# Block-causal attention and a gated MLP on one core: the posts of the v groups in another order

## The chip, the cores and the metric

The kernel runs on one core of a Trainium2 chip. The time is the device time of one execution in microseconds (us), as a median of several. The core has a matrix engine (TensorE, PE in the profile, with PEld for its weight loads), VectorE (DVE), ScalarE (ACT), GpSimd (POOL) and SyncE (SP), which issues most DMAs. Every engine works through its own list of instructions in order and waits on semaphores for the others.

## The reference

Attention over 8 batches, 8 heads, 576 tokens, 64 columns a head, with a mask by blocks of 64; its output, heads joined to 512 columns, goes through a gated MLP:

```python
scores = where(block_i >= block_j, q @ k.T / 8, -1e9)
attn = softmax(scores)                        # exp(s - max) / (sum + 1e-9)
x = join_heads(attn @ v)                      # 576 x 512 a batch
h = maximum(x @ w_in, 0)                      # 576 x 1024
u, v = h[..., :512], h[..., 512:]
v_n = (v - mean(v)) / sqrt(var(v) + 1e-6)     # by token
v_s = w_spatial @ v_n + b_spatial             # 576 x 576, over tokens
out = (u * v_s) @ w_out                       # 512 x 512
```

## The kernel before

Two heads make a pair, so a batch has four pairs (`pr` 0 to 3), and the program has 32 (`g`). The attention of one batch and the MLP of the batch before it are woven together. For each pair the main loop first issues all scores (L592, `scores_run`), which VectorE masks and takes the maximum of (L416), ScalarE exponentiates (`p`, L423) and GpSimd scales (L514); then the product with v of the pair before (`av_pair`, L676), which ScalarE casts and VectorE splits into high and low parts (`x`, L327 and L329). VectorE transposes p in blocks (`pb`, L631 and L638), and SP's DMAs regroup them into `ptt` (L652, L660) for the next `av`. Rows 512 and up of both heads make set 8 (L444 to L495).

Between these stand groups of the MLP, seven or eight to a pair. Matrix products use numbers split in two, so a product is three passes. The groups:

- `v_group(c)`, c from 0 to 4: the matmuls (`mv`, L719, for c = 4 L730), the emptying of the PSUM bank (`vr`, L724), then posts. The posts are the variance (L741, L742), on ScalarE 1/sqrt by Ln and Exp (L744, L745), four small products one column wide that polish it and give the shift (L747, L751, L755, L759, tile `st`), and last the scaling of `vr` (L764), its high part `vh` (L770) and on GpSimd its low part `vl` (L771). For c = 4 the parts are `vs_a` and `vs_b` (L776 to L778).
- `u_group`: the matmuls `mu` (L791) and the bank's emptying (L796).
- `sp_group`: `ms` (L821 to L826), which needs all `vh` and `vl`; then `out_group`: `mo` (L847).

A group is a Python generator. `issue` starts a new one, which emits its matmuls and empties its bank, and calls `follow`, which gives every group in the list `behind` one more step up to its next `yield`. So the `yield`s and the calls of `follow` set the place of the posts in every engine's list. From step 28 on, `issue` starts the new group first and calls `follow` after it. At the last group of pairs 0 and 1 `issue` leaves `follow` out, and it is called once between the products of the next pair's `av` and the transposes (L1049). What has been emitted is then chained with `in_order`, so each engine's list is exactly the order of emission.

The groups by pair, in batches 2 to 7 (the MLP is then that of the batch before): pair 0 has the last four `mo` and v0, v4, u; pair 1 has v1, u, v2, u, v3, u, u; pair 2 has the last three u and four `ms`; pair 3 four `mo` and four `ms`. In the MLP of batch 0 and in that of the last batch, which has no attention beside it, the order is another.

PSUM banks of tag `m` are two and serve all MLP groups in turn; six others in a ring (`bank`) serve scores and `av`. Of `vr` there are three buffers. `pb` and `ptt` are single.

Of the kernel before, what the change touches and what calls it, by code (L numbers as in the profile page):

```python
# [55 lines left out]
def kernel(  # L56
# [10 lines left out]
    nc = tc.nc  # L67
    B, NPAIR = qk.shape[0], qk.shape[1]
# [7 lines left out]
    FULL = S // P  # L76
# [98 lines left out]
    step = 0  # L175
# [342 lines left out]
    def scores_8(b, pr):  # L518
        raw = raws[(b, pr)]
        st = stats[(b, pr)] = st_p.tile([P, 52], F32, tag="sst", name=f"sst_{b}_{pr}", bufs=3)  # L520
        ps = [bank(f"s8_{b}_{pr}_{hd}") for hd in range(2)]
        matmuls_8(raw, ps)
        top_8(st, ps)
        yield
        norm_8(st)
        yield
# [50 lines left out]
    def scores_run(b, pr):  # L577


        raw = raws.pop((b, pr))  # L580
        st = stats.pop((b, pr))
        ps = {}
        for t in (3, 2, 1, 0):
            for hd in range(2):
                js = slice(64 * hd, 64 * hd + 64)
                n = P * (t + 1)
                if t:
                    bk = bank(f"s{t}_{b}_{pr}_{hd}")
                    ps[(t, hd)] = bk[:, :n]
                    if t == 1:  # L590
                        ps[(0, hd)] = bk[:, n:n + P]
                mm(  # L592
                    ps[(t, hd)], raw[js, S + t * P:S + (t + 1) * P], raw[js, :n],
                    start=True, stop=True,
                )
        due = None
        for ts in ((3,), (2,), (1, 0)):
            tiles = []
            for hd in range(2):
                p = (p_big if ts[0] == 3 else p_small)(f"p{ts[0]}_{b}_{pr}_{hd}")  # L600
                at = 0
                for t in ts:
                    n = P * (t + 1)
                    p_of[(b, pr, t, hd)] = p[:, at:at + n]
                    top(st, t, hd, p[:, at:at + n], [ps[(t, hd)]])
                    tiles.append((t, hd, p[:, at:at + n]))
                    at += n
            if due:
                norm(st, due)
            due = tiles  # L610
        turn_blocks(b, pr, 8, 0)
        turn_blocks(b, pr, 3, 0)
        norm(st, due)
# [84 lines left out]
    def moe(b):  # L698
# [10 lines left out]
        def v_group(c):  # L709
            ps = ps_m.tile([P, 512], F32, tag="m", name=f"mv_{b}_{c}")  # L710
            vr = ff_p.tile([P, DH], F32, tag="vr", name=f"vr_{b}_{c}", bufs=3)
            st = st_p.tile([P, 16], F32, tag="st", name=f"st_{b}_{c}")
            cs = slice(c * P, min((c + 1) * P, S))
            n = 0
            if c < FULL:
                m = P
                for k in range(NC):
                    for j, w in ((0, wi_hi), (0, wi_lo), (1, wi_hi)):
                        mm(  # L719
                            ps, xs[k][:, j, cs], w[:, k, DH:],  # L720
                            start=(n == 0), stop=(n == 3 * NC - 1),
                        )
                        n += 1
                nc.scalar.activation(vr, ps, AF.Relu)  # L724
            else:

                m = S - FULL * P
                for k in range(NC):
                    for w in (wi_hi, wi_lo):
                        mm(  # L730
                            ps, xs_tail[:, k].rearrange("p j t -> p (j t)"), w[:, k, DH:],
                            start=(n == 0), stop=(n == 2 * NC - 1),
                        )
                        n += 1
                nc.scalar.copy(vr[:m, :], ps[m:2 * m, :])
                nc.vector.tensor_tensor(out=vr[:m, :], in0=ps[:m, :], in1=vr[:m, :], op=ALU.add)
                nc.vector.tensor_scalar(
                    out=vr[:m, :], in0=vr[:m, :], scalar1=0.0, scalar2=None, op0=ALU.max
                )
            yield  # L740
            nc.vector.bn_stats(out=st[:m, 0:6], in_=vr[:m, :])  # L741
            nc.vector.bn_aggr(out=st[:m, 6:8], in_=st[:m, 0:6])  # L742
            yield
            nc.scalar.activation(st[:m, 8:9], st[:m, 7:8], AF.Ln, bias=eps[:m, :])  # L744
            nc.scalar.activation(st[:m, 9:10], st[:m, 8:9], AF.Exp, scale=-0.5)  # L745
            yield
            nc.vector.tensor_scalar(  # L747
                out=st[:m, 10:11], in0=st[:m, 7:8], scalar1=EPS_LN, scalar2=-0.5,
                op0=ALU.add, op1=ALU.mult,
            )  # L750
            nc.vector.tensor_scalar(  # L751
                out=st[:m, 11:12], in0=st[:m, 9:10], scalar1=st[:m, 9:10], scalar2=st[:m, 10:11],
                op0=ALU.mult, op1=ALU.mult,
            )
            nc.vector.tensor_scalar(  # L755
                out=st[:m, 12:13], in0=st[:m, 11:12], scalar1=1.5, scalar2=st[:m, 9:10],
                op0=ALU.add, op1=ALU.mult,
            )
            nc.vector.tensor_scalar(  # L759
                out=st[:m, 13:14], in0=st[:m, 6:7], scalar1=st[:m, 12:13], scalar2=-1.0,  # L760
                op0=ALU.mult, op1=ALU.mult,
            )
            yield
            nc.scalar.activation(  # L764
                vr[:m, :], vr[:m, :], AF.Identity, bias=st[:m, 13:14], scale=st[:m, 12:13]
            )
            if c < FULL:
                vh = ff_p.tile([P, DH], F32R, tag=f"vh{c}", name=f"vh_{b}_{c}")
                vl = ff_p.tile([P, DH], F32R, tag=f"vl{c}", name=f"vl_{b}_{c}")
                nc.scalar.copy(vh, vr)  # L770
                nc.gpsimd.tensor_tensor(  # L771
                    out=vl, in0=vr, in1=vh.bitcast(F32), op=ALU.subtract
                )
                vn[c] = (vh, vl)
            else:
                nc.vector.tensor_copy(vs_b[:m, :], vr[:m, :])  # L776
                nc.scalar.copy(vs_a[:m, :], vr[:m, :])
                nc.vector.tensor_tensor(  # L778
                    out=vs_a[64:64 + m, :], in0=vr[:m, :], in1=vs_b[:m, :].bitcast(F32),
                    op=ALU.subtract,  # L780
                )
# [17 lines left out]
        g = {}  # L799
# [112 lines left out]
    def next_step():  # L912
        nonlocal step
        for f in steps.pop(step, []):
            f()
        step += 1
        in_order()
# [37 lines left out]
    for n, (g, ts) in enumerate(sets):  # L955
# [21 lines left out]
        for f, tg in due:  # L977
            e = f(*pairs[tg], ps_m.tile([P, 512], F32, tag="m", name=f"av_{tg}"))
# [40 lines left out]
    behind = []  # L1019

    def follow():

        for e in list(behind):
            if next(e, e) is e:
                behind.remove(e)

    def issue(f, last=False):

        gen = f()
        if not last and step < 28:  # L1030
            follow()
        next(gen)
        if not last and step >= 28:
            follow()
        behind.append(gen)
        next_step()
# [3 lines left out]
    for g in range(NPAIR, len(pairs)):  # L1040
        b, pr = pairs[g]
        if g > NPAIR:
            scores_run(b, pr)
            av = av_pair(*pairs[g - 1])
            next(av, None)
            turn_blocks(b, pr, 3, 1)
            next(av, None)
            next(av, None)
            follow()  # L1049
            turn_blocks(b, pr, 2, 0)  # L1050
        regroup_8(b, pr)
        in_order()
        if pr == 0:
            if g > NPAIR:
                mlp = moe(b - 1)
            groups, rest = rest + mlp[0], mlp[-1]
        else:
            groups = mlp[pr]
        ahead = scores_8(*pairs[g + 1]) if g + 1 < len(pairs) else iter([])
        for i, f in enumerate(groups):  # L1060
            issue(f, pr < 2 and i == len(groups) - 1)
            if i == 0:
                turn_blocks(b, pr, 1, 0)
                turn_blocks(b, pr, 0, 0)
                turn_blocks(b, pr, 2, 1)
                turn_blocks(b, pr, 1, 1)
                turn_blocks(b, pr, 0, 1)
            if i == 1:
                regroup(b, pr)
            if i >= len(groups) - (4 if pr == 0 and g > NPAIR else 3):  # L1070
                next(ahead, None)
        in_order()
        if g + 1 < len(pairs):
            load_v(*pairs[g + 1])
        if g + 2 < len(pairs):
            load_pair(*pairs[g + 2])
        in_order()
# [61 lines left out]
```

## Time and profile before

| | us |
|---|---|
| median of 3 runs | 686.53 (686.02 to 687.38) |
| profiled execution | 685.92 |
| its span, first to last instruction | 683.8 |
| PE busy | 658.2 (96%) |
| DVE, ACT, POOL busy | 489.1, 390.3, 284.4 |
| one middle batch (309.56 to 389.76) | 80.20 |

A row of the timeline gives start, duration, engine, line, operation, output and inputs, shapes, count, and in brackets the engine's idle time before it with what ended it. `PE mu L791 <- ACT u L796: 5.1, 7, 2.8` in the list of waits reads: PE stood still before matmuls of line 791 until line 796 on ScalarE was done, 5.1 us in all, seven times, 2.8 us at the longest. The rows on the middle batch come from the MLP of batch 3, woven with the attention of batch 4.

### The profile page before, as it was taken

How to read it: one execution, taken by the hardware profiler on the slowest of the kernel's cores; microseconds unless marked ns; L12 is line 12 of the kernel's file. 1: busy time of each engine (PE TensorE's matmuls, PEld its weight loads, DVE VectorE, ACT ScalarE, POOL GpSimd, SP SyncE). 2: the span in 40 equal slices, each digit the busy share in tenths (PEclk: the TensorE clock that was granted, in tenths of full speed). 3: DMA queues.
4: the chain of work that ended last, by engine and by line, in shares of the span. 5: the costliest groups of instructions: out<-in, count | busy, mean ns of one | idle time of the engine just before them, and what ended most of it. 6: DMA issues, size and time to landing. Idle time of an engine off the chain costs nothing.

```text
span 683.8 us, 15564 instructions
## 1 busy us (share of the span) xinstructions
PE 658.2 (96%) x5328; PEld 554.3 (81%) x5328; DVE 489.1 (72%) x1899; ACT 390.3 (57%) x1144; POOL 284.4 (42%) x472
## 2 busy tenths in 40 slices
PE   8888889999999999999999999999999999999998
PEld 5545778888888887987789888888888887899998
DVE  6989898778966687776866788666877668661520
ACT  5877775456744476555654557534765556542632
POOL 4768566443443245442253434433354423540130
PEclk9999999999999999999999999999999999999999
DMA  6534664674557744566555545576445665442002
GB/s 234 169 136 151 193 145 121 179 184 112 134 137 180 180 109 102 154 165 160 140 133 141 149 125 146 132 185 174 95 110 157 152 173 150 111 112 62 0 1 70
DMA packets 51106, 93.45 MB, mean 137 GB/s; under 512 B 5970, under 2 KB 27986, under 8 KB 51028
## 3 DMA queue, kind: packets, MB, share of 16 engines
q1 hardware_dynamic: 41812, 83.03, 47.3%
q10 hardware_dynamic: 9216, 9.44, 4.2%
q8 instruction: 42, 0.69, 0.4%
q14 instruction: 36, 0.29, 0.1%
HBM read 37.13 MB, written 9.44 MB: 68 GB/s over the span
## 4 chain that ended last, share of the span: by engine, by line
PE 62%; DVE 22%; ACT 6%; POOL 5%; issue 3%; DMA 1%; SPq 0%; DVEq 0%; POOLq 0%; ACTq 0%
PE mo L847 15%; PE ms L821 13%; PE mv L719 8%; PE s L592 6%; PE mu L791 6%; PE av L676 5%; DVE p L416 4%; DVE pb L638 3%; POOL vl L771 3%; PE s L444 2%; PE mv L730 2%; POOL p L514 2%; DVE x L329 2%; ACT vr L764 2%; ACT vh L770 1%
## 5 line engine op out<-in xcount | busy, mean ns | idle before, releaser
L514 POOL TENSOR_SCALAR p<-p,sst 128x256 f32<-128x256 f32 (+4 forms) x244 | 130.3, 550 | 109.1 <-DVE sst L511 87.7
L423 ACT ACTIVATE p<-p,sst 128x256 f32<-128x256 f32 (+4 forms) x244 | 134.7, 554 | 40.6 <-DVE sst L416 40.5
L791 PE MATMUL mu<-x,wi_hi 128*128 128x288 f32 x512 | 112.3, 302 | 5.1 <-ACT u L796 5.1
L791 PEld LDWEIGHTS mu<-x,wi_hi 128*128 128x128 f32 x512 | 85.6, 191 | 11.2 <-ACT u L796 6.7
L416 DVE CUSTOM_DVE_ANT_0 p<-s,mask 128x512 f32<-128x512 f32 (+1 forms) x216 | 92.5, 484 | 1.3 <-PE s L592 0.7
L638 DVE STREAM_TRANSPOSE pb<-p 128x384 f32<-128x384 f32 (+1 forms) x224 | 90.0, 444 | 0.3 <-POOL p L514 0.3
L719 PE MATMUL mv<-wi_hi,x 128*128 128x512 f32 x256 | 86.8, 401 | 2.3 <-DVE x L329 1.0
L832 POOL TENSOR_TENSOR gl<-u,gh 128x288 fp32r<-128x288 f32 x45 | 36.1, 802 | 108.5 <-ACT gh L831 108.5
L828 DVE TENSOR_TENSOR u<-ms,u 128x288 f32<-128x288 f32 x64 | 29.2, 456 | 71.9 <-PE ms L826 71.9
L771 POOL TENSOR_TENSOR vl<-vr,vh 128x512 fp32r<-128x512 f32 x32 | 41.1, 1285 | 92.5 <-ACT vh L770 92.5
L821 PE MATMUL ms<-ws_hi,vl 128*128 128x288 f32 x256 | 76.4, 299 | 3.1 <-POOL vl L771 3.1
L821 PE MATMUL ms<-ws_hi,vh 128*128 128x288 f32 x256 | 77.1, 301 | 0.7 <-DVE u L828 0.7
L821 PE MATMUL ms<-ws_lo,vh 128*128 128x288 f32 x256 | 75.6, 295 | 0.0
L791 PE MATMUL mu<-x,wi_lo 128*128 128x288 f32 x256 | 70.4, 297 | 0.0
L676 PE MATMUL av<-ptt,v 128*64 128x64 f32 (+3 forms) x896 | 67.5, 303 | 2.1 <-DVE sst L416 2.1
L676 PEld LDWEIGHTS av<-ptt,v 128*64 128x64 f32 x896 | 53.4, 137 | 15.8 <-DVE sst L416 2.5
L592 PE MATMUL s<-raw 64*128 64x384 f32 (+3 forms) x432 | 65.5, 443 | 0.0
L719 PEld LDWEIGHTS mv<-wi_hi,x 128*128 128x128 f32 x256 | 48.0, 188 | 17.2 <-ACT o L853 2.6
L592 PEld LDWEIGHTS s<-raw 64*128 64x128 f32 x432 | 39.5, 187 | 25.4 <-issue 14.5
L484 ACT ACTIVATE p<-p,sst 128x288 f32<-128x288 f32 x56 | 29.5, 528 | 53.5 <-DVE sst L469 53.5
L853 ACT COPY o<-mo 128x288 f32<-128x288 f32 x64 | 25.5, 398 | 59.6 <-PE mo L847 54.8
L831 ACT CAST gh<-u 128x288 fp32r<-128x288 f32 x60 | 24.3, 428 | 59.6 <-DVE u L828 59.6
(157 smaller groups left out, 1471.9 us busy)
## 6 DMA issues: line engine op xcount, KB each, us to landing
ptt<-pb SPq DMA_DIRECT2D x112, 320.0 KB, 6.0
raw<-qk SPq DMA_DIRECT2D x31, 576.0 KB, 6.4
v<-v SPq DMA_DIRECT2D x32, 320.0 KB, 5.1
outT<-o ACTq DMA_DIRECT2D x64, 144.0 KB, 2.6
ptt<-pb SPq DMA_DIRECT2D x112, 80.0 KB, 2.3
r_gh<-w_in SPq DMA_DIRECT2D x3, 512.0 KB, 4.0
r_gl<-w_in SPq DMA_DIRECT2D x3, 512.0 KB, 3.5
rs<-w_spT SPq DMA_DIRECT2D x4, 288.0 KB, 4.3
```

The lines of the kernel that those rows point to most:

```text
L416: nc.vector.tensor_tensor_reduce(out=p[:, at:at + n], in0=ps, in1=mk, scale=-0.125, scalar=BIG if m == 0 else st[:, k:k + 1], op0=ALU.add, ...
L423: nc.scalar.activation(p, p, AF.Exp, bias=mx, scale=-1.0, accum_out=st[:, 10 + k:11 + k])
L514: nc.gpsimd.tensor_scalar(out=p, in0=p, scalar1=st[:, k:k + 1], scalar2=1.0, op0=ALU.mult, op1=ALU.mult)
L592: mm(ps[(t, hd)], raw[js, S + t * P:S + (t + 1) * P], raw[js, :n], start=True, stop=True,)
L638: nc.vector.transpose(to(hd * XH + 32 * t, [[96, m], *dims] if m > 1 else dims), p[:, :m * P])
L676: mm(to[js, :, 32 * c:], vt[:, c, js], ptt[:, 2 * z:2 * z + 2, at:at + P - 32 * c], start=(c == 0), stop=(c == 3),)
L719: mm(ps, xs[k][:, j, cs], w[:, k, DH:], start=(n == 0), stop=(n == 3 * NC - 1),)
L771: nc.gpsimd.tensor_tensor(out=vl, in0=vr, in1=vh.bitcast(F32), op=ALU.subtract)
L791: mm(ps[:, :HT], w[:, k, ds], xs[k][:, j, zs], start=(n == 0), stop=(n == 3 * NC - 1),)
L821: mm(ps[:, :HT], a[:, ds], w[:, k, zs], start=(n == 0), stop=False)
L832: (nc.vector if dc == ND - 1 else nc.gpsimd).tensor_tensor(out=gl[:, dc, :], in0=uz, in1=gh[:, dc, :].bitcast(F32), op=ALU.subtract)
L847: mm(ps[:, :HT], w[:, k, es], a[:, k, :], start=(n == 0), stop=(n == 3 * ND - 1),)
```

## The change

Four edits. The four small products of the fourth v group (c = 3) follow its Ln and Exp in the same step, without a `yield` between, in all batches but the first; in batches 1 to 6 they run on GpSimd instead of VectorE. From step 28 on, `follow` goes through `behind` from its end, so groups issued later emit their post first. The call of `follow` between the scores and the transposes is left out for the third pair (`pr` 2). And the last group of pair 1 now has its `follow`, from the third batch on, so that these posts stand ahead of the third pair's scores.

```diff
             nc.scalar.activation(st[:m, 9:10], st[:m, 8:9], AF.Exp, scale=-0.5)
-            yield
-            nc.vector.tensor_scalar(
+            if b == 0 or c != FULL - 1:
+                yield
+            small = nc.gpsimd if 0 < b < B - 1 and c == FULL - 1 else nc.vector
+            small.tensor_scalar(
                 out=st[:m, 10:11], in0=st[:m, 7:8], scalar1=EPS_LN, scalar2=-0.5,
                 op0=ALU.add, op1=ALU.mult,
             )
...
     def follow():
-        for e in list(behind):
+        for e in behind[::-1] if step >= 28 else list(behind):
             if next(e, e) is e:
                 behind.remove(e)
...
             next(av, None)
             next(av, None)
-            follow()
+            if pr != 2:
+                follow()
             turn_blocks(b, pr, 2, 0)
...
         for i, f in enumerate(groups):
-            issue(f, pr < 2 and i == len(groups) - 1)
+            issue(f, pr < 2 and i == len(groups) - 1 and not (pr and g > NPAIR + 1))
```

The other three small products change from `nc.vector` to `small` in the same way. The lists of PE and of SP are the same instructions in the same order as before. The others move; the rows are those of the MLP of batch 3, in which the changed kernel's lines from 747 on are higher by two.

ScalarE around the third pair's scores, before. `vr_2` and `vh_2` are the third v group, `st_3` the fourth's statistics, `p_4_2_…` the third pair's exponentials, `x` the casts behind `av`:

```order
L796 ACTIVATE u_4158<-mu_1_0_4429 128x288
L423 ACTIVATE p_4_2_0_4461,sst_2_4387<-p_4_2_0_4461,sst_2_4387 128x512
...
L327 CAST x_1_4511<-av_1_1_4516 128x320
L764 ACTIVATE vr_2_4323<-vr_2_4323,st_2_4324 128x512
L770 CAST vh_2_4539<-vr_2_4323 128x512
L744 ACTIVATE st_3_4366<-st_3_4366,eps 128x1
L745 ACTIVATE st_3_4366<-st_3_4366 128x1
L796 ACTIVATE u_4158<-mu_1_1_4551 128x288
L796 ACTIVATE u_4158<-mu_1_2_4574 128x288
L764 ACTIVATE vr_3_4365<-vr_3_4365,st_3_4366 128x512
L770 CAST vh_3_4589<-vr_3_4365 128x512
```

and now:

```order
L798 ACTIVATE u_4158<-mu_1_0_4429 128x288
L744 ACTIVATE st_3_4366<-st_3_4366,eps 128x1
L745 ACTIVATE st_3_4366<-st_3_4366 128x1
L766 ACTIVATE vr_2_4323<-vr_2_4323,st_2_4324 128x512
L772 CAST vh_2_4450<-vr_2_4323 128x512
L423 ACTIVATE p_4_2_0_4472,sst_2_4387<-p_4_2_0_4472,sst_2_4387 128x512
...
L327 CAST x_1_4522<-av_1_1_4527 128x320
L798 ACTIVATE u_4158<-mu_1_1_4555 128x288
L766 ACTIVATE vr_3_4365<-vr_3_4365,st_3_4366 128x512
L772 CAST vh_3_4570<-vr_3_4365 128x512
L798 ACTIVATE u_4158<-mu_1_2_4579 128x288
```

Four posts have moved from behind the casts to ahead of the exponentials, and the fourth group's last posts from behind the second u to ahead of it.

GpSimd around the same scores, before (`p_96` is set 8, `xs` the tail of x):

```order
L495 TENSOR_SCALAR p_96<-p_96,sst_2_4387 128x288 x2
L514 TENSOR_SCALAR p_4_2_0_4461<-p_4_2_0_4461,sst_2_4387 128x512
...
L514 TENSOR_SCALAR p_4_2_1_4482<-p_4_2_1_4482,sst_2_4387 128x128
L342 TENSOR_SCALAR xs_4229<-x_1_4511 128x128
L771 TENSOR_TENSOR vl_2_4540<-vr_2_4323,vh_2_4539 128x512
L771 TENSOR_TENSOR vl_3_4590<-vr_3_4365,vh_3_4589 128x512
```

and now:

```order
L495 TENSOR_SCALAR p_96<-p_96,sst_2_4387 128x288 x2
L749 TENSOR_SCALAR st_3_4366<-st_3_4366 128x1
L753 TENSOR_SCALAR st_3_4366<-st_3_4366 128x1
L757 TENSOR_SCALAR st_3_4366<-st_3_4366 128x1
L761 TENSOR_SCALAR st_3_4366<-st_3_4366 128x1
L773 TENSOR_TENSOR vl_2_4451<-vr_2_4323,vh_2_4450 128x512
L514 TENSOR_SCALAR p_4_2_0_4472<-p_4_2_0_4472,sst_2_4387 128x512
...
L514 TENSOR_SCALAR p_4_2_1_4493<-p_4_2_1_4493,sst_2_4387 128x128
L342 TENSOR_SCALAR xs_4229<-x_1_4522 128x128
L773 TENSOR_TENSOR vl_3_4571<-vr_3_4365,vh_3_4570 128x512
```

The four products are new here, and `vl_2` has moved ahead of the third pair's eight p.

VectorE ahead of these scores, before:

```order
L747 TENSOR_SCALAR st_4_4131<-st_4_4131 64x1
...
L759 TENSOR_SCALAR st_4_4131<-st_4_4131 64x1
L741 BN_STATS st_1_4268<-vr_1_4267 128x6
L742 BN_AGGR st_1_4268<-st_1_4268 128x2
L776 CAST vs_b<-vr_4_4130 64x512
L778 TENSOR_TENSOR vs_a<-vr_4_4130,vs_b 64x512
L747 TENSOR_SCALAR st_1_4268<-st_1_4268 128x1
...
L759 TENSOR_SCALAR st_1_4268<-st_1_4268 128x1
L741 BN_STATS st_2_4324<-vr_2_4323 128x6
L742 BN_AGGR st_2_4324<-st_2_4324 128x2
L477 ISA p_96,sst_2_4387<-s_4_2_0_4388,mask 128x288
```

and now:

```order
L741 BN_STATS st_1_4268<-vr_1_4267 128x6
L742 BN_AGGR st_1_4268<-st_1_4268 128x2
L749 TENSOR_SCALAR st_4_4131<-st_4_4131 64x1
...
L761 TENSOR_SCALAR st_4_4131<-st_4_4131 64x1
L778 CAST vs_b<-vr_4_4130 64x512
L780 TENSOR_TENSOR vs_a<-vr_4_4130,vs_b 64x512
L741 BN_STATS st_2_4324<-vr_2_4323 128x6
L742 BN_AGGR st_2_4324<-st_2_4324 128x2
L749 TENSOR_SCALAR st_1_4268<-st_1_4268 128x1
...
L761 TENSOR_SCALAR st_1_4268<-st_1_4268 128x1
L477 ISA p_96,sst_2_4387<-s_4_2_0_4388,mask 128x288
```

The statistics of the later group stand ahead of the products of the earlier one. Behind the transposes the four products of `st_3` are gone from VectorE.

More of the change, by code (lines that the diff above doesn't have):

```diff
@@ L750, in v_group @@
             )
-            nc.vector.tensor_scalar(
+            small.tensor_scalar(
                 out=st[:m, 11:12], in0=st[:m, 9:10], scalar1=st[:m, 9:10], scalar2=st[:m, 10:11],
@@ L754, in v_group @@
             )
-            nc.vector.tensor_scalar(
+            small.tensor_scalar(
                 out=st[:m, 12:13], in0=st[:m, 11:12], scalar1=1.5, scalar2=st[:m, 9:10],
@@ L758, in v_group @@
             )
-            nc.vector.tensor_scalar(
+            small.tensor_scalar(
                 out=st[:m, 13:14], in0=st[:m, 6:7], scalar1=st[:m, 12:13], scalar2=-1.0,
```

## The prediction

> **What bounds the kernel now.** I read the page first, then the core by stretches, then the waits of TensorE alone, then the timelines of one batch. Busy time by engine:
>
> ```profile
> PE 658.2 (96%) x5328; PEld 554.3 (81%) x5328; DVE 489.1 (72%) x1899; ACT 390.3 (57%) x1144; POOL 284.4 (42%) x472
> ```
>
> TensorE is busy for 96%. Nothing can come from the other engines except through a hole on PE. Six batches in the middle repeat. One of them, by stretch; then, over the whole run, the two waits of PE that recur (us in total, times, longest):
>
> ```profile
> 309.56:389.76 80.20, 79.27 (x665) 67.76 (x665) 59.69 (x240) 45.36 (x137) 31.40 (x54) 1.00 0.57 144
> ```
>
> ```profile
> PE mu L791 <- ACT u L796: 5.1, 7, 2.8
> ...
> PE ms L821 <- POOL vl L771: 3.1, 7, 0.5
> ```
>
> The clock granted is 1.00, and PE is idle for 80.20 - 79.27 = 0.93 us of the batch. Each wait comes seven times: once in each middle batch (0.38 and 0.47 in the one below; 6 x 0.38 + 2.8 = 5.1, 6 x 0.47 + 0.2 = 3.0), the 2.8 once in batch 0, where the change leaves ScalarE's order as it is, and the 0.2 once in the last batch. The ends of matmuls are modelled, so I take the price of each hole from starts. PE's timeline of this batch (start us, us, engine, line):
>
> ```profile
> 339.50 2.40 PE L676 MATMUL av<-ptt,v 128*64 128x256 f32 x32
> ...
> 345.18 0.69 PE L791 MATMUL mu<-x,wi_hi 128*128 128x288 f32 x4
> 346.24 0.40 PE L791 MATMUL mu<-x,wi_hi 128*128 128x288 f32 x1 [0.38 <-ACT u L796]
> 346.48 0.29 PE L791 MATMUL mu<-x,wi_lo 128*128 128x288 f32 x1
> ...
> 349.15 0.30 PE L821 MATMUL ms<-ws_hi,vh 128*128 128x288 f32 x1
> 349.28 0.29 PE L821 MATMUL ms<-ws_lo,vh 128*128 128x288 f32 x1
> 350.05 0.40 PE L821 MATMUL ms<-ws_hi,vl 128*128 128x288 f32 x1 [0.47 <-POOL vl L771]
> 350.29 0.30 PE L825 MATMUL ms<-ws_a,vs_a 128*128 128x288 f32 x1
> ...
> 359.45 2.40 PE L676 MATMUL av<-ptt,v 128*64 128x256 f32 x32
> ```
>
> Without a wait these matmuls start 0.13 us apart (349.15, 349.28). Four from 345.18 bring the next to 345.71; it starts at 346.24, and its successor comes 0.24 later instead of 0.13. The first hole costs 0.53 + 0.11 = **0.64 us**. The second: 349.28 + 0.13 = 349.41, actual 350.05, again with 0.24 behind it: 0.64 + 0.11 = **0.75 us**. The first is a PSUM bank: the fourth u group of the second half needs the one that L796 empties. The second is vl of the fourth v group.
>
> **The change part by part.** ScalarE and GpSimd on that stretch:
>
> ```profile
> 337.25 0.41 ACT L796 ACTIVATE u<-mu 128x288 f32<-128x288 f32 x1 [0.30 <-PE mu L791]
> 339.04 0.72 ACT L423 ACTIVATE p<-p,sst 128x512 f32<-128x512 f32 x1 [1.39 <-DVE sst L416]
> ...
> 343.42 0.67 ACT L327 CAST x<-av 128x256 fp32r<-128x256 f32 x2
> 343.99 0.82 ACT L764 ACTIVATE vr<-vr,st 128x512 f32<-128x512 f32 x1
> ...
> 345.37 0.29 ACT L744 ACTIVATE st<-st,eps 128x1 f32<-128x1 f32 x1
> ...
> 345.80 0.69 ACT L796 ACTIVATE u<-mu 128x288 f32<-128x288 f32 x2
> ```
>
> ```profile
> 338.45 0.98 POOL L495 TENSOR_SCALAR p<-p,sst 128x288 f32<-128x288 f32 x2 [1.90 <-DVE sst L469]
> 341.15 2.52 POOL L514 TENSOR_SCALAR p<-p,sst 128x512 f32<-128x512 f32 x4 [1.72 <-DVE sst L511]
> 344.54 1.63 POOL L514 TENSOR_SCALAR p<-p,sst 128x256 f32<-128x256 f32 x4 [0.88 <-DVE sst L511]
> ...
> 346.40 1.29 POOL L771 TENSOR_TENSOR vl<-vr,vh 128x512 fp32r<-128x512 f32 x1
> 348.72 1.27 POOL L771 TENSOR_TENSOR vl<-vr,vh 128x512 fp32r<-128x512 f32 x1 [1.03 <-ACT vh L770]
> ```
>
> **Posts moved ahead of the third pair's scores.** vr_2, vh_2 (343.99 to 345.37, 1.38 us) and the Ln and Exp of st_3 (345.37 to 345.80, 0.43) leave the place behind the casts of x and go behind the u of 337.25. There ScalarE had a hole of 1.39. 1.81 goes in, so 0.42 sticks out: the exponentials start at 339.46, they and the casts end at 343.99 + 0.42 = 344.41, and u comes there instead of at 345.80, 1.39 sooner. PE wants that bank at 345.71. The **first hole closes** with 0.9 to spare (0.39 for the u itself): 0.64 per batch. Cover gone, it costs nothing until the exponentials are 0.9 later still.
>
> **GpSimd.** It now does p of set 8 (0.98), four products of st_3, vl_2, then the eight p, xs, vl_3. The products are not in the trace. The nearest rows:
>
> ```profile
> L514 POOL TENSOR_SCALAR p<-p,sst 128x128 f32<-128x128 f32 x60 | 22.7, 379 | 0.0
> L342 POOL TENSOR_SCALAR xs<-x 128x128 fp32r<-128x128 f32 x32 | 9.5, 298 | 2.0 <-DVE x L329 2.0
> ...
> L107 POOL MEMSET eps<- 128x1 f32 x1 | 0.1, 98 | 0.0
> ```
>
> Below: four at 0.10 and no gap, 0.4. Above: four at 0.38 with 0.2 between dependent ones, 2.1. I take 1.25: by width, 128x512 to 128x128 falls by some 0.1 per 128 columns, so a width of 1 is some 0.27 with a pointer scalar and 0.19 without, and 0.08 for each of three waits. From 338.45, 0.23 later for VectorE (below): 338.68 + 0.98 + 1.25 + 1.29 = 342.20, where the first four p start (341.15 before), to 344.72. The last four wait for L511, 0.42 later as the exponentials are: 344.96 to 346.55, xs to 346.82. vh_3 stands right behind u on ScalarE now: 344.41 + 0.33 + 1.38 = 346.1, so it no longer ends the wait. vl_3 runs 346.82 to 348.10. PE wants it at 349.41 - 0.64 = 348.77, its weight load 0.13 sooner. The **second hole closes** with 0.5 to spare: 0.75 per batch.
>
> **VectorE.** Rows:
>
> ```profile
> 330.86 0.42 DVE L776 CAST vs_b<-vr 64x512 fp32r<-64x512 f32 x1 [1.02 <-ACT vr L764]
> ...
> 338.31 0.69 DVE L416 CUSTOM_DVE_ANT_0 p<-s,mask 128x512 f32<-128x512 f32 x1
> 338.92 0.08 DVE L416 DVE_READ_ACCUMULATOR2_ANT sst<- 128x1 f32 x1
> ...
> 343.39 0.53 DVE L638 STREAM_TRANSPOSE pb<-p 128x384 f32<-128x384 f32 x1
> ...
> 346.15 0.11 DVE L747 TENSOR_SCALAR st<-st 128x1 f32<-128x1 f32 x1
> ...
> 347.05 1.61 DVE L638 STREAM_TRANSPOSE pb<-p 128x256 f32<-128x256 f32 x5
> ```
>
> **Later groups first** puts Ln and Exp of st_1 ahead of vr_4 on ScalarE, 0.43, so vs_b starts 0.43 later; VectorE is full from there to L416. L416 is later by 0 to 0.43; I take 0.23, because the product behind each aggregate now belongs to another group and need not wait for it. That matters at one place: av of 339.50 writes the bank that the first L416 reads, whose accumulator comes at 339.00, so up to 0.45 fits, and at worst 0.05 per batch is lost. The transposes wait for p, which GpSimd brings 1.05 later: the first is done at 342.20 + 2.52 / 4 = 342.8, and VectorE reaches it at 343.39 + 0.42 = 343.8. So they move by 0.42, and the products' 0.90 (346.15 to 347.05) is gone from among them. They end at 347.05 + 1.61 - 0.48 = 348.2.
>
> The Trainium skill (GPSIMD Engine Reference, section 3, Performance versus the Vector engine) speaks against moving small arithmetic to GpSimd: it gives 1.96 times VectorE's time for an elementwise operation of two inputs. On VectorE's 0.90 for the four that would be an estimated 1.8 in place of 1.25; no run here shows it. By that rule nothing would be left of the 0.5 to spare: the sum would be the same by a hair, and the first rival below likelier.
>
> The last transfer that follows the transposes, as SP's queue issues it, and its way to landing:
>
> ```profile
> 351.85 1.96 SPq L660 DMA_DIRECT2D ptt<-pb  x1
> ...
> DMA to landing us min/median/max: 6.1/6.1/6.1
> ```
>
> It lands at 357.95. The second half of the av of 359.45 needs it half of 2.40 later, at 360.6, now 359.2: 1.2 to spare even at the old issue time. SP gets nothing new, and no DMA is moved past another.
>
> **Last batch and batch 0.** The last batch has the second hole alone, and batch 0 one in which av waits for L416:
>
> ```profile
> 653.85 0.29 PE L821 MATMUL ms<-ws_lo,vh 128*128 128x288 f32 x1
> 654.31 0.40 PE L821 MATMUL ms<-ws_hi,vl 128*128 128x288 f32 x1 [0.16 <-POOL vl L771]
> ...
> 96.00 1.28 POOL L771 TENSOR_TENSOR vl<-vr,vh 128x512 fp32r<-128x512 f32 x1 [1.43 <-ACT vh L770]
> 96.68 0.89 DVE L776 CAST vs_b<-vr 64x512 fp32r<-64x512 f32 x1
> ...
> 103.54 2.40 PE L676 MATMUL av<-ptt,v 128*64 128x256 f32 x32 [0.33 <-DVE sst L416]
> ```
>
> The former costs 0.46 - 0.13 + 0.11 = 0.44 and goes, since vr_3 now stands ahead of u and its products come at once. In batch 0 the same vs_b took 0.89 against 0.42, with GpSimd's vl_3 running beside it until 97.28. vr_4 now comes ahead of vr_3, so vl_3 comes later and vs_b is free: 0.45 less on a full VectorE, and the 0.33 before av goes (0 to 0.45).
>
> **Sum:** 6 x (0.64 + 0.75) + 0.44 + 0.33 = 9.1 us. The profiled execution took 685.9 (span 683.8); it lies 0.6 under the median of 686.5. The span becomes 674.7, that execution's time 676.8, the median **677.4**.
>
> **The rivals.**
> *Only the first hole closes.* If GpSimd's four products take 2.4 us (0.6 each), vl_3 is 1.15 later than above and the 0.75 stays: 677.4 + 4.5 = 681.9. For it: a chain of dependent one-column products on GpSimd is nowhere in the trace. Against it: a product 128 columns wide takes 0.38.
> *The time is given back at the fourth pair's av.* If the eight p behind vl_2 hold the transposes, L660 comes late and av waits for ptt. To eat 1.39 it must land 2.6 later than now. Only the ends stay gained: 686.5 - 0.8 = 685.7, no change. Against it: GpSimd's p were never the last thing the transposes waited for in this pair.
> *Slower.* The same GpSimd queue, dearer: vl_2, eight p and vl_3 all stand behind the products. From 0.76 us each (3.0 in all) the wait for vl_3 takes more than both holes gave; at 1.0 each (4.24 with gaps) vl_3 is 2.5 late, costs 2.60 per batch against 1.39 gained, 686.5 + 6 x 1.21 - 0.8 = 693.0. Only the unknown price speaks for it; the one-input rows of GpSimd above are at half that or under.
>
> **How the numbers follow.** Forecast 0.73, only the first hole 0.13, given back 0.08, slower 0.06. About 0.2% (1.4 us) is what a measurement of this kernel can tell from no change. Faster: 0.73 + 0.13 = 0.86; same 0.08; slower 0.06. The forecast's own range: 676.3 (av in batch 0 gives 0.45 and later waits there shrink too) to 680.3 (products at 2.1, then 0.37 + 0.11 per batch is lost). With the first rival: 676.2 to 682.8, which leaves out 0.14 and the forecast's own tails.
>
> **What would show it.** Right: the line PE mu <- ACT u and the line PE ms <- POOL vl vanish from PE's waits in the middle batches; the batch is 78.8 instead of 80.2; u starts some 1.4 sooner after the scores; vl_2 on GpSimd ends before the third pair's p begin; PE busy stays 658. Wrong: PE still waits for vl (GpSimd's products dear, to be read from their pitch), a new wait of av for L416 (VectorE later than 0.45) or for ptt.

## The result and the profile after

| | before | after |
|---|---|---|
| median of four runs each, us | 686.59 (686.02 to 687.38) | 677.13 (676.89 to 678.82) |
| span of the profiled execution | 683.8 | 675.2 |
| one middle batch | 80.20 | 78.84 |
| PE busy | 658.2 (96%) | 655.9 (97%) |

The ratio is 0.9867 (95% interval 0.9848 to 0.9885): the changed kernel is 1.3% faster. 677.4 was forecast, from 676.2 to 682.8.

The page of the changed kernel, the longest of its waits of PE over the whole run (us in total, times, longest), and the middle batch that answers to the one in the prediction, by stretch:

```profile
PE 655.9 (97%) x5328; PEld 554.2 (82%) x5328; DVE 482.9 (72%) x1875; ACT 390.8 (58%) x1144; POOL 291.1 (43%) x496
```

```profile
PE mu L793 <- ACT u L798: 3.4, 2, 2.8
```

```profile
306.74:385.58 78.84, 78.76 (x665) 67.66 (x665) 58.78 (x236) 45.42 (x137) 32.51 (x58) 1.00 0.58 146
```

The line PE ms behind POOL vl is gone. The line PE mu behind ACT u counts two where it counted seven, and both lie in batch 0. In the middle batch PE now idles for 0.08 us of 78.84, where it idled for 0.93 of 80.20. Over the run PE's idle time falls by 6.3 us (25.6 to 19.3) and its busy time by 2.3.

For the experiments I measure a middle batch between two rows that return once per batch, the scores of set 8 for the second pair. In before and in after they are:

```profile
308.84 0.72 PE L444 MATMUL s<-raw 64*64 64x288 f32 x8
...
389.04 0.72 PE L444 MATMUL s<-raw 64*64 64x288 f32 x8
```

```profile
306.02 0.72 PE L444 MATMUL s<-raw 64*64 64x288 f32 x8
...
384.86 0.72 PE L444 MATMUL s<-raw 64*64 64x288 f32 x8
```

Between the two, the changed kernel's lead grows from 2.82 to 4.18 us: 1.36 in one batch. Over the run it grows from 0.10 behind batch 0 to 8.16 at the last scores of set 8 of the program, six steps of 1.34 in the mean, and the rest of the program gives 0.46 more.

Now the stretch itself. When the third pair's scores begin the changed kernel is 2.80 us ahead (334.34 against 337.14), so 2.80 is added to these times to compare them with those of the prediction. PE, ScalarE, GpSimd and VectorE after:

```profile
342.38 0.83 PE L793 MATMUL mu<-x,wi_hi 128*128 128x288 f32 x5
...
343.98 0.70 PE L793 MATMUL mu<-x,wi_hi 128*128 128x288 f32 x4
344.52 0.29 PE L823 MATMUL ms<-ws_hi,vh 128*128 128x288 f32 x1
...
345.98 0.30 PE L823 MATMUL ms<-ws_hi,vl 128*128 128x288 f32 x1
```

```profile
336.54 0.72 ACT L423 ACTIVATE p<-p,sst 128x512 f32<-128x512 f32 x1
...
341.51 0.41 ACT L798 ACTIVATE u<-mu 128x288 f32<-128x288 f32 x1
341.82 0.81 ACT L766 ACTIVATE vr<-vr,st 128x512 f32<-128x512 f32 x1
```

```profile
336.92 0.19 POOL L749 TENSOR_SCALAR st<-st 128x1 f32<-128x1 f32 x1
...
338.24 1.29 POOL L773 TENSOR_TENSOR vl<-vr,vh 128x512 fp32r<-128x512 f32 x1
339.50 4.18 POOL L514 TENSOR_SCALAR p<-p,sst 128x512 f32<-128x512 f32 x8
343.63 0.31 POOL L342 TENSOR_SCALAR xs<-x 128x128 fp32r<-128x128 f32 x1
343.89 1.32 POOL L773 TENSOR_TENSOR vl<-vr,vh 128x512 fp32r<-128x512 f32 x1
```

```profile
335.70 0.69 DVE L416 CUSTOM_DVE_ANT_0 p<-s,mask 128x512 f32<-128x512 f32 x1
...
343.15 2.06 DVE L638 STREAM_TRANSPOSE pb<-p 128x384 f32<-128x384 f32 x6
```

No row of PE has a wait in brackets any more, and vl of the fourth group is done at 345.21, 0.77 before the matmul of 345.98 that reads it.

### The profile page after: what moved, and what is told of

It reads as the page before. It is cut to its first block, busy times and chain, and to the rows that moved or that the text cites. A ratio compares the mean times of both kernels' runs of the same rounds, so it can differ in the third digit from the quotient of the medians.

```text
span 675.2 us, 15538 instructions
## 1 busy us (share of the span) xinstructions
PE 655.9 (97%) x5328; PEld 554.2 (82%) x5328; DVE 482.9 (72%) x1875; ACT 390.8 (58%) x1144; POOL 291.1 (43%) x496
## 4 chain that ended last, share of the span: by engine, by line
PE 74%; DVE 14%; ACT 5%; POOL 3%; issue 2%; SPq 1%; DMA 1%; DVEq 0%; ACTq 0%; POOLq 0%
PE mo L849 16%; PE ms L823 15%; PE mu L793 11%; PE mv L719 8%; PE s L592 8%; PE av L676 7%; DVE p L416 2%; PE s L444 2%; PE mv L730 2%; PE av L688 2%; DVE pb L638 1%; ACT p L423 1%; PE ms L828 1%; PE ms L827 1%; DVE x L329 1%
## 5 line engine op out<-in xcount | busy, mean ns | idle before, releaser
L793 PE MATMUL mu<-x,wi_hi 128*128 128x288 f32 x512 | 110.9, 300 | 3.4 <-ACT u L798 3.4
L416 DVE CUSTOM_DVE_ANT_0 p<-s,mask 128x512 f32<-128x512 f32 (+1 forms) x216 | 92.5, 484 | 1.3 <-PE s L592 0.7
L855 ACT COPY o<-mo 128x288 f32<-128x288 f32 x64 | 25.6, 399 | 59.3 <-PE mo L849 53.5
```

Of the source, the lines that this page charges most:

```text
L416: nc.vector.tensor_tensor_reduce(out=p[:, at:at + n], in0=ps, in1=mk, scale=-0.125, scalar=BIG if m == 0 else st[:, k:k + 1], op0=ALU.add, ...
L793: mm(ps[:, :HT], w[:, k, ds], xs[k][:, j, zs], start=(n == 0), stop=(n == 3 * NC - 1),)
```

## The experiments

| kernel | median, us | ratio to before (95%) | middle batch, us |
|---|---|---|---|
| calls of follow moved, nothing else | 688.18 | 1.0014 (1.0002 to 1.0026) | 80.42 |
| products in one step on GpSimd, nothing else | 708.48 | 1.0315 (1.0281 to 1.0350) | 82.63, some 84.2 |
| change without "later first" | 678.95 and 679.36 | 0.9877 and 0.9885 | 78.83 |
| change with the products on VectorE | 681.37 | 0.9912 (0.9891 to 0.9932) | 79.54 |
| change | 677.13 and 678.38 | 0.9867 and 0.9868 | 78.84 and 78.83 |
| change, four more products | 682.06 | 0.9929 (0.9914 to 0.9943) | 79.47 |
| change, eight more products | 696.68 | 1.0140 (1.0125 to 1.0156) | 80.90 or 82.4 |
| change, own buffer for vr_4 | 675.35 | 0.9827 (0.9811 to 0.9844) | 78.50 |
| change, u first in batch 0 | 677.73 | 0.9864 (0.9850 to 0.9879) | 78.84 |
| both of these | 674.84 | 0.9817 (0.9795 to 0.9839) | 78.49 |

**The products on VectorE.**

```diff
-            small = nc.gpsimd if 0 < b < B - 1 and c == FULL - 1 else nc.vector
+            small = nc.vector
```

> The changed kernel, but the four small products of the fourth v group stay on VectorE (still in one step with Ln and Exp). On VectorE they then stand right ahead of the third pair's first L416. My theory (VectorE had only some 0.3 us to spare there, GpSimd had the room): L416 0.92 us later, the av behind it waits 0.6 to 0.7 us in each of six batches, both old holes stay closed, so 677.1 + 4 = 681 us. Rival (the engine does not matter, only the place of the posts): 677.1 us, no wait of av for L416 in the middle batches.

Measured: 681.37, batch 79.54, 0.70 longer than with GpSimd. VectorE's first L416 of the third pair and the av behind it:

```profile
338.69 0.21 DVE L757 TENSOR_SCALAR st<-st 128x1 f32<-128x1 f32 x1
338.94 0.21 DVE L761 TENSOR_SCALAR st<-st 128x1 f32<-128x1 f32 x1
339.07 0.68 DVE L416 CUSTOM_DVE_ANT_0 p<-s,mask 128x512 f32<-128x512 f32 x1
```

```profile
339.81 2.40 PE L676 MATMUL av<-ptt,v 128*64 128x256 f32 x32 [0.64 <-DVE sst L416]
```

The products stand between the statistics and L416, and av waits for L416 in each of six batches. Both old holes stay closed. So the engine matters, and VectorE has no 0.9 us to spare at that place.

**Without "later groups first".**

```diff
-        for e in behind[::-1] if step >= 28 else list(behind):
+        for e in list(behind):
```

> The changed kernel without 'later groups first'. My theory: on GpSimd vl_2 then stands ahead of the four products instead of behind them, 1.3 us each, so the eight p begin at the same time, the exponentials too; vr_3 needs the products only some 2 us later. Middle batch the same within 0.1 us (78.85), the time 677.1 within 1 us. Rival (the reversal carries a part of the gain): a wait of PE comes back in the middle batches, 679 us or more.

Measured: 678.95, 1.8 above the changed kernel, outside the 1 us that I had allowed. (The two come from different series; by the ratios, each to before in its own series, it is 0.7, and the intervals overlap.) The middle batches are equal to 0.02 us (78.83), as expected, so the reversal carries nothing there. The difference lies ahead of them and behind them: this profile is 1.57 us late already at the end of batch 0's MLP, and the stretch behind the last set 8 is 88.5 us against 87.7. A second series, with the changed kernel and a third one beside it, was to tell a real difference from the spread of the start:

> The changed kernel again, unchanged, as the measure for the three beside it. 677.1 us; every theory expects the same.

> The changed kernel without 'later groups first' again. Its middle batches were as long as the changed kernel's (78.83 against 78.84 us), its time 1.8 us above. My theory (the reversal is worth something in batch 0 and at the end alone): 1 to 2 us above the changed kernel again. Rival (the start of the kernel, which differs by up to 1.4 us between profiles of the same program, made all of it): within 0.4 us of it.

```diff
-        for e in behind[::-1] if step >= 28 else list(behind):
+        for e in behind[::-1] if step >= 49 else list(behind):
```

> The changed kernel with the list reversed only behind the MLP of batch 0; apart from the MLP of batch 0 it is the changed kernel. The prediction's term for batch 0 (vs_b off GpSimd's way, the wait of av for L416 gone) says 0.33 us (0 to 0.45) above the changed kernel. Rival (the reversal matters more in batch 0 than that): 1 us or more above. Rival (nothing is left of it, since PE waits for another u instead): the same.

Measured: 678.38 for the change, 679.36 without the reversal, 678.37 with the reversal behind batch 0's MLP only. The whole reversal is worth about 1.0 us here. Some 0.4 of it may be the stretch behind the last set 8: 88.0 to 88.5 us in the five profiles without it (mean 88.2), 87.5 to 88.0 in the nine with it (mean 87.8). For batch 0 the two readings disagree. The medians see nothing (the single runs reach from 677.8 to 679.7). The profiles, from the av near 83 us to the row near 149, take 65.7 to 66.7 us in the six whose batch 0 is not reversed (mean 66.4) and 65.1 to 66.1 in the six with the changed kernel's order there (mean 65.7). Much of this spread is a spell in which PE runs at half its clock (the last section), which lies elsewhere from profile to profile. Where it has the same length and about the same place, the reversal takes off 0.6 us (66.69 twice against 66.09 and 66.05) or 0.9 to 1.0 (66.58 and 66.66 against 65.65 twice). What it is worth in the median, from nothing to 1.0 us, stays open.

**The calls of follow alone.**

```diff
-            if b == 0 or c != FULL - 1:
-                yield
-            small = nc.gpsimd if 0 < b < B - 1 and c == FULL - 1 else nc.vector
+            yield
+            small = nc.vector
```

and the list in its old order.

> Before, with the two edits on the calls of follow alone (products on VectorE, in a step of their own, old order in the list). My theory: the first hole (PE mu behind ACT u, 0.64 us per batch) closes, the second (PE ms behind POOL vl) stays and grows to about 1.0, since vr_3 still waits for products that stand among the transposes: 0.3 to 0.5 us per batch gained, 683.5 to 685 us. Rival (moving the posts ahead of the scores is all of it): 678 us. Rival (nothing without the products): 686.5 us.

Measured: 688.18, a batch of 80.42, 0.2 longer than before. A miss: I expected a gain. The first hole is closed, but the second has become two. PE, then ScalarE, then VectorE:

```profile
350.31 0.40 PE L822 MATMUL ms<-ws_hi,vh 128*128 128x288 f32 x1 [0.24 <-ACT vh L771]
351.66 0.40 PE L822 MATMUL ms<-ws_hi,vl 128*128 128x288 f32 x1 [0.82 <-POOL vl L772]
```

```profile
348.79 0.82 ACT L765 ACTIVATE vr<-vr,st 128x512 f32<-128x512 f32 x1 [1.07 <-DVE st L760]
```

```profile
347.36 0.56 DVE L638 STREAM_TRANSPOSE pb<-p 128x384 f32<-128x384 f32 x1
347.84 0.11 DVE L748 TENSOR_SCALAR st<-st 128x1 f32<-128x1 f32 x1
```

The products still stand among the transposes. These now come later, with the exponentials, and the ms are wanted 0.64 sooner, since the first hole is gone. vr_3 has nothing to wait for but the products. In the prediction a hole of 0.38 idle cost 0.64, so the idle time and about 0.26: 0.24 + 0.82 + 0.52 = 1.58, against 1.36 for the two old holes. I had expected about 1.0 for the second hole: I had put the products 0.6 us too early among the transposes.

**The products alone on GpSimd, in one step.** The other three edits taken back.

> Before, with the products alone moved to GpSimd into one step with Ln and Exp; the calls of follow and the order in the list as before. My theory: the products then stand on GpSimd behind the eight p and vl_2 (1.3 us later than on VectorE), vr_3 waits for them on ScalarE with the u of the third group of the half behind it, and PE waits for that bank about 2.1 us, besides the first hole of 0.64: 1.3 us per batch slower than before, 694 us. Rival (each edit gains its own hole): 682 us.

Measured: 708.48, a batch of 82.63, against 694 expected: a miss in size. GpSimd, ScalarE and PE:

```profile
354.13 0.19 POOL L749 TENSOR_SCALAR st<-st 128x1 f32<-128x1 f32 x1
```

```profile
355.54 0.81 ACT L766 ACTIVATE vr<-vr,st 128x512 f32<-128x512 f32 x1 [3.00 <-POOL st L761]
...
356.91 0.71 ACT L798 ACTIVATE u<-mu 128x288 f32<-128x288 f32 x2
```

```profile
357.36 0.40 PE L823 MATMUL ms<-ws_hi,vh 128*128 128x288 f32 x1 [2.91 <-ACT u L798]
```

The mechanism is the expected one: GpSimd comes to the products only behind the p and vl_2, ScalarE waits 3.00 us for them with two u behind, and PE waits 2.91 us for the bank. I had said 2.1: I left out the emptying itself (356.91 to 357.36); where the other 0.4 comes from is not shown. Six times the 2.43 that a batch is longer would make 701.5; besides, some batches take 84.2 us, of which the last section tells.

**How much room vl_3 has.**

```diff
+            if 0 < b < B - 1 and c == FULL - 1:
+                for _ in range(4):
+                    nc.gpsimd.tensor_scalar(
+                        out=st[:m, 14:15], in0=st[:m, 11:12], scalar1=1.5,
+                        scalar2=st[:m, 9:10], op0=ALU.add, op1=ALU.mult,
+                    )
             yield
```

> The changed kernel with four more products on GpSimd behind the four (into a column nobody reads), in the same six batches: the queue ahead of vl_2, the eight p and vl_3 gets some 1.2 us longer. My theory (vl_3 has about 0.6 us to spare): PE waits for vl about 0.6 to 0.7 us per batch, 677.1 + 4 = 681 us. Rival (there is no more than 0.2 to spare): 683 us or more. Rival (vl_3 is not what a late GpSimd delays, the transposes and ptt are): a wait of av for a DMA.

> The same with eight more, some 2.4 us. My theory: each further us goes straight into the wait for vl, some 1.8 to 1.9 us per batch, 677.1 + 11 = 688 us, about the point where the change turns to a loss. Rival (part of it is hidden by the av and the scores that follow): under 684 us.

GpSimd's added products, vl_3 and the matmul that reads it, and the waits of PE in the middle of the run, with four; then products and waits with eight:

```profile
340.05 1.36 POOL L767 TENSOR_SCALAR st<-st 128x1 f32<-128x1 f32 x4
...
346.95 1.30 POOL L779 TENSOR_TENSOR vl<-vr,vh 128x512 fp32r<-128x512 f32 x1
```

```profile
348.31 0.40 PE L829 MATMUL ms<-ws_hi,vl 128*128 128x288 f32 x1 [0.39 <-POOL vl L779]
```

```profile
PE ms L829 <- POOL vl L779: 2.3, 6, 0.4
```

```profile
181.08 2.80 POOL L767 TENSOR_SCALAR st<-st 128x1 f32<-128x1 f32 x8
```

```profile
PE ms L829 <- POOL vl L779: 10.8, 6, 1.8
```

Four cost 0.63 us per batch, as expected, and the whole kernel 682.06. Counted from the start of the third pair's scores (334.34 in the changed kernel, 336.12 here), vl_3 ends 1.26 later (12.13 against 10.87) and its matmul starts 0.55 later (12.19 against 11.64), so vl_3 had 0.71 to spare. With eight it ends 2.68 later and the matmul starts 1.96 later: 0.72 again. Beyond that, work costs its own length: 1.44 us more of it with eight than with four, and 1.43 more per batch (2.06, in the batches that take 80.90, against 0.63). Six times 2.06 would make 689.5, near the 688 expected. But the other batches with eight take 82.4, which nobody expected: four of six, some 6 us together, and so the kernel takes 696.68.

**A third small hole.** In the changed kernel ScalarE waits 1.41 us before it empties the third v group's bank, since it takes over the buffer of the first group, which is free only when that group's vl is done:

```profile
326.71 0.60 ACT L724 ACTIVATE vr<-mv 128x512 f32<-128x512 f32 x1 [1.41 <-POOL vl L773]
```

```diff
-            vr = ff_p.tile([P, DH], F32, tag="vr", name=f"vr_{b}_{c}", bufs=3)
+            if b and c == FULL:
+                vr = ff_p.tile([P, DH], F32, tag="rw", name=f"vr_{b}_{c}")
+            else:
+                vr = ff_p.tile([P, DH], F32, tag="vr", name=f"vr_{b}_{c}", bufs=3)
```

> The changed kernel, with the fifth v group's vr in another buffer (from the second batch on), so that the third v group need not wait for the first one's vl to be done. In the profile of after ScalarE waits 1.41 us for POOL vl before it empties the third group's bank, and mv of the fourth group starts 0.24 + 0.10 late. My theory: these 0.34 us per batch go, 677.1 - 2.0 = 675.1 us, middle batch 78.5. Rival (PE would only wait a little later for the next post): 677 us.

Measured: 675.35, batch 78.50. The 0.34 per batch is gone as forecast. ScalarE now waits for the matmuls alone:

```profile
326.04 0.60 ACT L727 ACTIVATE vr<-mv 128x512 f32<-128x512 f32 x1 [0.44 <-PE mv L722]
```

**The long wait of batch 0.**

```diff
-        if not last and step < 28:
+        if not last and step < 27:
             follow()
         next(gen)
-        if not last and step >= 28:
+        if not last and step >= 27:
             follow()
```

> The changed kernel, with one post moved in the MLP of batch 0: the third u empties its bank ahead of Ln and Exp of two v groups instead of behind them. PE stands still for 2.80 us there and then runs some 2.6 us at a lower granted clock. My theory: the wait goes, but VectorE has no idle time in this stretch and sets the av behind it through L416, so only 0.4 to 0.9 us of the end is gained: 676.5 us. Rival (PE's stall and the low clock after it are worth their length): 2.8 + 1.2 = 4 us, 673 us.

Measured: 677.73, no gain in the median. PE's wait of 2.8 us has split:

```profile
90.96 0.40 PE L793 MATMUL mu<-x,wi_hi 128*128 128x288 f32 x1 [0.56 <-ACT u L798]
...
94.33 0.40 PE L793 MATMUL mu<-x,wi_hi 128*128 128x288 f32 x1 [1.51 <-ACT u L798]
...
100.09 0.40 PE L793 MATMUL mu<-x,wi_hi 128*128 128x288 f32 x1 [1.49 <-ACT u L798]
```

That is 3.56 us in three waits, and no low clock behind them; the changed kernel waits there for 2.80 and 0.65, in its second profile for 2.79 and 1.00. The rival, 4 us gained, is out: what PE does not wait for here it waits for later. From the av near 83 us to the row near 149, which leaves the start out, this kernel takes 65.08 us and the changed one 65.65 and, in its second profile, 65.08. That VectorE sets this stretch fits (here it is busy for 11.5 of the 12 us from 88 to 100), but it was not tested apart.

> The changed kernel with both further moves: vr of the fifth group in another buffer (2.0 us by the middle batches, 78.49 against 78.84) and in batch 0 the third u ahead of Ln and Exp (which took away the 2.8 us wait of PE and the low clock behind it, but gave no shorter time by itself). My theory: 675 us, the second adds 0 to 0.6. Rival (they hinder each other): 677 us.

Measured: 674.84, the shortest of all, 1.8% under before. Against the own buffer alone (675.35 in another series; the ratios are 0.9817 and 0.9827) the second move can't be told from nothing.

## Why the prediction was right, step by step

*What bounds the kernel.* Right. PE's two holes per batch were put at 0.64 + 0.75 = 1.39; the batch lost 1.36. One sign of being right did not come: PE busy was to stay 658 and fell to 655.9. The prices themselves speak against it: they count 0.11 us of each hole behind the start of the matmul that waited, which takes 0.40 us in place of 0.29, so 1.4 us for the thirteen holes.

*The sum.* 9.1 us were forecast; the profiled spans differ by 8.6 (8.06 in the six batches, 0.46 at the end, 0.10 in batch 0), the medians by 9.5 and, in the second series, by 9.1. That the median came within 0.3 us of the forecast is partly luck: single runs of the changed kernel reach from 676.89 to 678.82, and its second series has a median of 678.38.

*The way there.* Forecast, and measured with 2.80 added:

| | forecast | measured |
|---|---|---|
| first L416 | 338.54 | 338.50 |
| exponentials begin | 339.46 | 339.34 |
| u emptied from | 344.41 | 344.31 |
| four products to vl_2, us | 1.25 | 1.32 |
| vl_3 begins | 346.82 | 346.69 |
| transposes end | 348.2 | 348.01 |

So the gain came the way that was said: the u 1.49 sooner (345.80 before), vl_3 some 2 us sooner (348.72 before), at the price of a GpSimd queue and a VectorE that had the room.

*The price of the products.* It was the unknown, and taken between 0.4 and 2.1 at 1.25 by extending GpSimd's widths. The groups of one-column products of the changed kernel from 140 to 640 us, GpSimd and VectorE (total us, mean ns):

```profile
L753 POOL TENSOR_SCALAR st<-st 128x1 f32<-128x1 f32 x6 | 2.0, 338 | 0.6
L757 POOL TENSOR_SCALAR st<-st 128x1 f32<-128x1 f32 x6 | 1.6, 267 | 0.6
L761 POOL TENSOR_SCALAR st<-st 128x1 f32<-128x1 f32 x6 | 1.6, 262 | 0.6
L749 POOL TENSOR_SCALAR st<-st 128x1 f32<-128x1 f32 x6 | 1.2, 192 | 0.5
```

```profile
L753 DVE TENSOR_SCALAR st<-st 128x1 f32<-128x1 f32 x21 | 5.7, 273 | 1.8
L761 DVE TENSOR_SCALAR st<-st 128x1 f32<-128x1 f32 x21 | 4.5, 214 | 0.7
L757 DVE TENSOR_SCALAR st<-st 128x1 f32<-128x1 f32 x21 | 4.5, 214 | 0.8
L749 DVE TENSOR_SCALAR st<-st 128x1 f32<-128x1 f32 x22 | 2.6, 117 | 0.0
```

The extension gave 0.27 for the three with a pointer and 0.19 for the one without: measured 0.26 to 0.34, and 0.19. Between two of them lie 0.09 to 0.11 us, where 0.08 had been taken without a row to show it. Four take 1.06 us on GpSimd and 0.82 on VectorE, 1.29 times as long. The Trainium skill (GPSIMD Engine Reference, section 3, Performance versus the Vector engine) has 1.96 times, for an operation of two inputs on wide tiles; at one column this trace does not bear that out, and the measurement decides.

*The last batch.* 0.44 forecast; the stretch from the last scores of set 8 to the issue of the last output is 88.14 before and 87.68 after, 0.46, and PE's wait for vl in it is gone. Over all profiles this stretch spreads by 0.5 us in one order, so the size is good to a few tenths only.

*Batch 0.* "vl_3 comes later and vs_b is free ... and the 0.33 before av goes" has the mechanism right. In all six profiles without the reversal there vs_b takes 0.88 to 0.90 us and av waits 0.13 to 0.54 for L416; in all eight with it vs_b takes 0.41 and av does not wait. But the size can't be read from the first two profiles: by the end of batch 0 the change has gained 0.10 in them, not 0.33. In after another wait stands ahead of av:

```profile
99.72 0.40 PE L793 MATMUL mu<-x,wi_hi 128*128 128x288 f32 x1 [0.65 <-ACT u L798]
```

The reversal does not make it: two profiles without the reversal have it too, 0.64 us long, and there av waits 0.53 and 0.54 besides. Its length changes with the place of the half clock. In both kernels PE runs at half its clock for 3.4 us near the end of the 2.8 us wait (91.9), in before from 93.2 on, in after from 91.5 on. Two stretches of 2 us, first in before, then in after:

```profile
92.00:94.00 2.00, 2.00 (x13) 2.00 (x14) 1.86 (x9) 1.25 (x3) 0.98 (x2) 0.79 0.40 138
94.00:96.00 2.00, 2.00 (x10) 2.00 (x9) 1.75 (x8) 1.88 (x4) 0.57 (x1) 0.50 0.60 67
```

```profile
92.00:94.00 2.00, 2.00 (x9) 2.00 (x10) 1.86 (x8) 1.21 (x3) 1.03 (x2) 0.50 0.33 113
94.00:96.00 2.00, 2.00 (x14) 2.00 (x14) 1.82 (x8) 0.91 (x2) 0.53 (x1) 0.78 0.62 69
```

After, the low clock fell on the first of two mu groups, so that its u came at 95.09 in place of 94.09, and all of ScalarE's list behind it, the u of 99.27 too, came 0.9 later. A term of a third of a us can't be read from one profile of this stretch; what the reversal is worth there is open, as told above.

*The rivals.* Neither the first nor the last was near: both needed products of 0.6 us and more, and they took 0.33 with their gaps. Their mechanism is real, as the eight added products show, but "2.4 us in all, and the 0.75 stays" was too dear: vl_3 had 0.7 us to spare, not 0.5. Nothing was given back at the fourth pair's av in the middle batches; no profile has a wait of av for ptt in all six.

*What the prediction did not say* is that the parts don't gain apart. It gave each hole to a part of the change, 0.64 to the posts ahead of the scores, 0.75 to the products on GpSimd. Alone, the moved calls make the kernel 0.14% slower and the products 3.15%. The products can go to GpSimd only if they stand ahead of the p there, which the moved call of follow brings; and that call pays only if the products leave their place among the transposes. In one step with Ln and Exp, the whole change brings 0.9% with them on VectorE and 1.3% with them on GpSimd.

## What to carry to other kernels

Moving a post sooner pays when its whole chain moves: the link left behind, here four products of 0.1 to 0.3 us among the transposes, becomes the new wait, and its price counts from the moment at which the consumer wants it once the other hole is closed. Replay each engine's new list with the old durations and with the new demand times; here that gave the times of a stretch of 10 us within 0.2, but in the two experiments with half of the change it missed by 0.6 and 0.8. An engine that is slower by some 30% but idle was the better place here for a chain of tiny operations, as long as the queue behind them has room; measure the room by adding work until it shows.

## What was not expected of the hardware

A stall of PE can cost more than its length. Near the end of some stalls the granted clock falls to 0.50. In the fourteen profiles there are 21 such spells ahead of PE's last matmul: sixteen last 3.42 to 3.44 us, five last 6.84, twice that. They begin between 0.9 us before the end of the stall and 1.4 us behind it. With eight added products, behind the wait that ends at 190.76, then around the same wait one batch later, which ends at 273.18:

```profile
191.20:194.20 3.00, 3.00 (x14) 3.00 (x14) 0.46 (x1) 0.43 (x1) 0.80 (x1) 0.50 0.92 146
...
273.00:276.00 3.00, 2.82 (x25) 2.51 (x25) 0.70 (x2) 0.43 (x1) 0.93 (x2) 1.00 0.69 111
```

In 3 us PE has 14 matmuls in place of 25, and the batch takes 82.4 in place of 80.9. A spell came with four of six stalls of 1.8 us here, three of six of 2.9 us with the products alone on GpSimd, and eleven of the twelve of 2.8 us in batch 0. It came with none of the fourteen of 1.77 us at the av near 83, and none of the four of 1.5 us with the u first in batch 0; but with two of the fourteen of 1.27 us near 54 us and one of the fourteen of 0.92 us near 19, in the less busy start. So the length of the stall alone does not decide. The Trainium skill (TensorE: Matmul & The Clock Gate, section "HAM oscillation — how this bites in real kernels") warns of idle gaps of PE above about 3.4 us; in these runs 1.8 us and less were enough, though not each time. What decides between the one and the other was not tested.
